# Retention and two expert layers on one core: state product spread over four array quadrants, transposes as quadrant products, PSUM banks in fixed groups, five conversion buffers

## The chip, the core and the metric

The kernel runs on one core of one Trainium2 chip. The engines of the core are TensorE (PE in the profile; PEld is its weight load), VectorE (DVE), ScalarE (ACT), GpSimd (POOL) and SyncE (SP). Here SP only issues DMAs, and POOL issues a second kind of DMA that adds to what stands in memory. The metric is the device time of one execution in microseconds.

## The reference

Inputs are q, k, v of shape (2, 8, 768, 64): 2 sequences, 8 heads, 768 steps, 64 values per head. First comes a retention layer with a 64x64 state per head:

```
gamma = 1 - 2**(-5 - head)
for t in range(768):
    state = gamma * state + outer(k[t], v[t])
    y[t]  = (q[t] @ state) / sqrt(64)
```

Its output, as 1536 rows of 512 values, runs through two expert layers, each with its own weights (512x2048 and 2048x512):

```
h = x @ w_in ;  g = softplus(h)              ;  x = g @ w_out     # first
h = x @ w_in ;  g = h * clip(h+3, 0, 6) / 6  ;  out = g @ w_out   # second
```

q, k and v are 32-bit floats. The expert weights are 64-bit floats and are loaded as pairs of 32-bit words; the products are made in 32-bit formats.

## The kernel before

**Retention.** The 768 steps of a sequence are cut into chunks of 128; a chunk of a sequence is a unit, numbered 0 to 11 (units 0 to 5 are the first sequence). `attend(u)` issues these pieces for a unit, named after the table `cost`:

- Tk and Tq: k and q of the unit are turned so that the 64 values of a head lie on partitions. Two heads (a pair) share one 128x128 transpose, so 4 transposes for k and 4 for q. ACT copies the turned k out of its PSUM bank (`kT`), DVE multiplies the turned q by the decay table into `qT`.
- S: scores of each half chunk (64 steps), 16 products of 64x64 each; DVE masks them into `pt`.
- D: 16 products of k and the scaled v (`vs`) give what each half chunk adds to the state; DVE adds it up into the states `st` at the middle and at the end of the unit.
- C: what the carried state gives to each step, 16 products (8 in the first unit of a sequence). ACT copies the result (`e`).
- I: what the scores give, 16 products; DVE adds the copy of C to it (`g`), and ACT and DVE split the sum into a high and a low part (`x_hi`, `x_lo`) for the first expert layer.

The array of TensorE has 128 rows (partitions that are read) and 128 columns (partitions that are written), and a 64x64 product uses one quarter of it. The head h of a pair lies on partitions 0 to 63 or 64 to 127 by g = h % 2. In S and D the products go round all four quarters. In C before, the state of a head lies on half g and its output on the same half g, so C uses only the two quarters of the diagonal.

**Expert layers.** Both are cut into 3 chunks of 512 tokens and 16 slices of 128 hidden values. G1 of a slice makes h (12 matmuls of 128x512: high x high, high x low, low x high for each of 4 pieces), ACT and DVE make g and split it, and G2 of the slice adds into 4 accumulators (12 matmuls). G2 runs two slices behind G1. In all there are 96 G1 and 96 G2.

**Weights.** A slice's weight is converted once: SP loads its words into one of 3 `raw` buffers, ACT and DVE build the 32-bit value in a converted-word buffer `cv` (4 before), and ACT writes the high part to `w`. The low part comes in one of two ways. For weights chosen by `BY_DVE(n)` DVE subtracts high from full (`w<-cv,w` in the profile). For the others ACT first writes the negative and POOL starts a DMA that adds the full value to what stands in `w`; its `cv` buffer is held until that DMA has landed. The first 32 weights, for the first expert layer, are all needed for its first chunk of tokens.

**Order.** Class `Plan` holds every step as a task with an engine, a cost, its predecessors, a due time and the buffers that it takes and gives back. `Plan.run` simulates the engines with those costs and lays down each engine's instructions in the order that comes out; this order is then fixed, and each engine works through its own list. `spread` says between which G1 and G2 the pieces of units 4 to 11 are due: those of units 4 to 7 from the first G1 on, those of 8 to 11 from the second chunk of tokens on. The 8 PSUM banks are a pool: before, a task that takes two banks gets any two neighbours, other tasks any free ones.

Of the kernel before, what the change touches and what calls it, by code (L numbers as in the profile page):

```python
# [16 lines left out]
P = 128  # L17
# [5 lines left out]
class Plan:  # L23
# [20 lines left out]
    def __init__(self, tc):  # L44
        self.tc, self.tasks, self.pools, self.users, self.slot = tc, [], {}, {}, {}
        self.tensor, self.vector, self.scalar, self.gpsimd, self.sync = (
            self.Engine(self, getattr(tc.nc, e)) for e in ("tensor", "vector", "scalar", "gpsimd", "sync"))
# [13 lines left out]
    def places(self, pool, keys, at=None):  # L61

        times = [(x if at is None else max(x, at), i) for i, x in enumerate(self.pools[pool]) if x is not None]
        if len(keys) == 2:
            have = {i: x for x, i in times}
            two = min(((max(x, have[i + 1]), -i) for i, x in have.items() if i + 1 in have), default=None)
            return two and [-two[1], 1 - two[1]]
        return [i for _, i in sorted(times)[:len(keys)]] if len(times) >= len(keys) else None

    def run(self, log=None):  # L70
        free = {"PE": 0.0, "DVE": 0.0, "ACT": 0.0, "POOL": 0.0, "SP": 1.2}
        line = 0.0
# [52 lines left out]
def kernel(ctx, tc, q, k, v, w1_in, w1_out, w2_in, w2_out, tq, tk, tcc, out):  # L125
# [15 lines left out]
    RAW, CV, LD, LATE = 3, 4, 3, 8  # L141
# [3 lines left out]
    def BY_DVE(n):  # L145
        return n < 6 or n < 2 * NF and n % 3 == 1
# [29 lines left out]
    nc.pool("bank", 8)  # L176
    conv = [[("conv", m, i) for i in range(9)] for m in range(2)]
# [19 lines left out]
    cost = {"Tk": 0.46, "Tq": 0.46, "S": 0.60, "D": 0.60, "C": 0.98, "I": 0.60, "G1": GEMM, "G2": GEMM}  # L197
# [156 lines left out]
    def both(keys):  # L354
        a, b = sorted(nc.slot[x][1] for x in keys)
        return banks[:, a:b + 1:b - a, :NP * HALF].rearrange("p x (n t) -> p x n t", n=NP)

    def sub(keys, j):
        i = sorted(nc.slot[x][1] for x in keys)[j]
        return banks[:, i, :NP * HALF].rearrange("p (n t) -> p n t", n=NP)  # L360

    def bank(key):
        return at_slot(key).rearrange("p (n t) -> p n t", n=NP)
# [4 lines left out]
    def attend(u):  # L368
# [38 lines left out]

        def turned(n):
            def go():
# [4 lines left out]
        tp = task("PE", cost["Tk"], turned("k"), [ik], d["Tk"], take=[("bank", ("kP", u))])  # L414
        kt = task("ACT", ACP, lambda: nc.scalar.activation(tile_of("kT"), bank(("kP", u)), AF.Copy), [tp], d["S"] - 1.0,
                  take=own("kT"), give=[("kP", u)])
        tp = task("PE", cost["Tq"], turned("q"), [iq], d["Tq"], take=[("bank", ("qP", u))], give=[("q", u)])
        qt = task("DVE", PSX, lambda: nc.vector.tensor_tensor(tile_of("qT"), bank(("qP", u)), tq_sb, ALU.mult), [tp, tables["q"]],
                  d["S"] - 1.1, take=own("qT"), give=[("qP", u)])
# [6 lines left out]
        def scores():  # L426
            for p in range(NP):
                for j in range(2):
                    for g in range(2):
                        nc.tensor.matmul(sub(sc, g)[part[j], p, :], tile_of("kT")[part[g], p, part[j]], tile_of("qT")[part[g], p, part[j]])  # L430
# [3 lines left out]
            tile_of("pt").rearrange("p n (g t) -> p g n t", g=2).rearrange("p g n t -> p g n t"), both(sc),  # L434
# [5 lines left out]
        def product():  # L440
            for h in range(H):
                g, p = h % 2, h // 2
                for j in subs:
                    nc.tensor.matmul(sub(ds, j)[part[g], p, :], tile_of("k")[part[j], h, :], tile_of("vs")[part[j], h, :])
# [4 lines left out]
        def middle():  # L449
            if first:  # L450
                nc.vector.tensor_copy(at_slot(mid[1]), sub(ds, 0))
            else:
                nc.vector.tensor_tensor(at_slot(mid[1]), at_slot(("end", u - 1)), sub(ds, 0), ALU.add)
# [3 lines left out]
        if not last:  # L457
            def total():
                nc.vector.tensor_tensor(at_slot(end[1]), at_slot(mid[1]), sub(ds, 1), ALU.add)
# [7 lines left out]

        def carry():
            for j in range(int(first), 2):
                w = at_slot(mid[1] if j else ("end", u - 1))  # L470
                for p in range(NP):
                    for g in range(2):
                        nc.tensor.matmul(bank(("oc", u))[part[g], p, part[j]], w[part[g], p, :], tile_of("qT")[part[g], p, part[j]])

        c = task("PE", cost["C"] / (1 + first), carry, [qt, sm, None if first else ready["end", u - 1]], d["C"],
                 take=[("bank", ("oc", u))], give=[mid[1], ("qT", u)] + ([] if first else [("end", u - 1)]))

        def inner():
            for h in range(H):
                g, p = h % 2, h // 2  # L480
                for j in range(2):
                    nc.tensor.matmul(sub(oi, j)[part[g], p, :], tile_of("vs")[part[j], h, :], tile_of("pt").rearrange(
                        "p n (g t) -> p g n t", g=2)[part[j], g, p, :])
# [6 lines left out]
        def split(t):  # L490
            return t.rearrange("p n (j t) -> p j n t", j=2)

        def of(n):
            return at_slot((n, u)).rearrange("p (n t) -> p n t", n=NP)

        if first:
            o0 = task("ACT", 0.35, lambda: nc.scalar.activation(split(of("on"))[:, 0], sub(oi, 0), AF.Copy), [n], d["I"] + 0.7,
                      take=[("g", ("on", u))], give=oi)
            o1 = task("ACT", 0.35, lambda: nc.scalar.activation(split(of("oe"))[:, 1], split(bank(("oc", u)))[:, 1], AF.Copy), [c],
                      d["I"], take=[("e", ("oe", u))], give=[("oc", u)])  # L500
            on = task("DVE", 0.42, lambda: nc.vector.tensor_tensor(split(of("on"))[:, 1], split(of("oe"))[:, 1], sub(oi, 1), ALU.add),
                      [n, o0, o1], d["I"] + 1.0, give=oi + [("oe", u)])
        else:
            o1 = task("ACT", ACP, lambda: nc.scalar.activation(of("oe"), bank(("oc", u)), AF.Copy), [c],
                      d["I"], take=[("e", ("oe", u))], give=[("oc", u)])
# [115 lines left out]
def _tables(H, S, D):  # L621
# [4 lines left out]
    tq = np.repeat(up.reshape(H // 2, 2, 1, C), D, axis=2).reshape(H // 2, 2 * D, C).transpose(1, 0, 2)  # L626
    tk = gamma[None, :] ** -t[:, None]
    gc = np.repeat((gamma ** C).reshape(H // 2, 2, 1), D, axis=2).reshape(H // 2, 2 * D).T
# [27 lines left out]
```

## Time and profile before

| | |
|---|---|
| runs of the kernel before | 605.39, 607.04, 610.01 us (median 607.04) |
| profiled execution | 606.65 us, of which 604.5 us are the span of the trace |
| PE busy | 582.9 us (96%) |
| DVE, ACT busy | 335.9 us (56%), 304.7 us (50%) |
| granted TensorE clock, mean | 0.992 |

All steps are recorded through one helper, so the rows of the profile carry the line L41; groups are told apart by the tiles that they write and read. `ident,k` is Tk, `ident,q` Tq, `qT,kT` S, `vs,k` D, `qT,st` C and `pt,vs` I. From unit 8 on the tiles lie in the buffers of the weight conversion and are called `raw` and `cv` there: `ident,raw` is T, `cv,raw` D and S, `cv,st` C, `cv,cv` I. The profile counts a 64x64 or 64-column product twice (x32 for 16 products). The chain that ended last is three quarters PE.

### The profile page before, as it was taken

How to read it: one execution, taken by the hardware profiler on the slowest of the kernel's cores; microseconds unless marked ns; L12 is line 12 of the kernel's file. 1: busy time of each engine (PE TensorE's matmuls, PEld its weight loads, DVE VectorE, ACT ScalarE, POOL GpSimd, SP SyncE). 2: the span in 40 equal slices, each digit the busy share in tenths (PEclk: the TensorE clock that was granted, in tenths of full speed). 3: DMA queues.
4: the chain of work that ended last, by engine and by line, in shares of the span. 5: the costliest groups of instructions: out<-in, count | busy, mean ns of one | idle time of the engine just before them, and what ended most of it. 6: DMA issues, size and time to landing. Idle time of an engine off the chain costs nothing.

```text
span 604.5 us, 9654 instructions
## 1 busy us (share of the span) xinstructions
PE 582.9 (96%) x3891; PEld 478.2 (79%) x3891; DVE 335.9 (56%) x584; ACT 304.7 (50%) x516; POOL 44.3 (7%) x57
## 2 busy tenths in 40 slices
PE   7698889999999999999999999999999999999997
PEld 6576668878788888888888887888888888888886
DVE  4899898995655333376677985622422222322223
ACT  2468877994533333476779996622222222222220
POOL 0001111120000000011122221100000000000000
PEclk9899989999999999999999999999999999999999
DMA  8997776966210100046588987510100000100001
GB/s 193 237 252 199 195 183 158 241 180 137 54 37 21 51 0 1 1 105 157 152 196 212 247 211 176 130 18 0 71 1 1 0 1 0 71 0 1 0 1 69
DMA packets 68364, 59.87 MB, mean 99 GB/s; under 512 B 39776, under 2 KB 56416, under 8 KB 68320
## 3 DMA queue, kind: packets, MB, share of 16 engines
q1 hardware_dynamic: 61264, 46.41, 26.9%
q0 software_dynamic: 7056, 12.85, 12.4%
q8 instruction: 30, 0.49, 0.4%
q14 instruction: 14, 0.11, 0.1%
HBM read 43.26 MB, written 3.15 MB: 77 GB/s over the span
## 4 chain that ended last, share of the span: by engine, by line
PE 76%; DVE 10%; DMA 6%; ACT 5%; issue 3%; SPq 1%; DVEq 0%; ACTq 0%
PE banks L41 76%; DVE cv L41 5%; DMA raw<-in_moe_w_out_dram 3%; DMA raw<-in_moe_w_in_dram 2%; DVE raw L41 1%; ACT w L41 1%; DVE g L41 1%; DVE lo L41 1%; ACT raw L41 1%; DMA v<-in_v_dram 1%; ACT cv L41 1%; ACT e L41 1%; SPq L41 1%; DVE x_lo L41 1%; DVE w L41 1%
## 5 line engine op out<-in xcount | busy, mean ns | idle before, releaser
L41 PE MATMUL banks<-x_hi,w 128*128 128x512 f32 x768 | 254.8, 393 | 5.0 <-ACT kT L41 2.2
L41 PEld LDWEIGHTS banks<-x_hi,w 128*128 128x128 f32 x768 | 144.8, 189 | 37.1 <-DVE g L41 2.5
L41 PE MATMUL banks<-x_lo,w 128*128 128x512 f32 x384 | 150.2, 391 | 0.0
L41 PE MATMUL banks<-hi,w 128*128 128x512 f32 x384 | 127.5, 393 | 0.8 <-ACT w L41 0.5
L41 PE MATMUL banks<-w,hi 128*128 128x512 f32 (+1 forms) x386 | 118.3, 388 | 0.0
L41 DVE SCALAR_TENSOR_TENSOR g<-e,banks 128x512 f32<-128x512 f32 x48 | 33.0, 688 | 114.1 <-ACT e L41 114.0
L41 ACT ACTIVATE e<-banks,three 128x512 f32<-128x512 f32 x48 | 32.9, 686 | 124.6 <-PE banks L41 116.7
L41 DVE SCALAR_TENSOR_TENSOR cv<-raw,cv 128x512 uint32<-128x512 uint32 x128 | 87.5, 689 | 6.7 <-ACT cv L41 4.2
L41 DVE TENSOR_TENSOR lo<-g,hi 128x512 fp32r<-128x512 f32 x96 | 66.2, 690 | 44.7 <-ACT hi L41 43.4
L41 ACT ACTIVATE hi<-g 128x512 fp32r<-128x512 f32 x96 | 60.5, 630 | 49.8 <-DVE g L41 33.3
L41 PEld LDWEIGHTS banks<-hi,w 128*128 128x128 f32 x384 | 72.0, 188 | 17.0 <-ACT w L41 0.9
L41 PEld LDWEIGHTS banks<-x_lo,w 128*128 128x128 f32 x384 | 72.6, 189 | 14.7
L41 PEld LDWEIGHTS banks<-w,hi 128*128 128x128 f32 x386 | 72.4, 188 | 14.9
L41 ACT ACTIVATE w<-cv 128x512 fp32r<-128x512 f32 x113 | 68.3, 624 | 16.7 <-DVE cv L41 16.2
L41 PE MATMUL banks<-lo,w 128*128 128x512 f32 x192 | 75.1, 391 | 1.4 <-DVE lo L41 1.4
L41 PE MATMUL banks<-w,lo 128*128 128x512 f32 (+1 forms) x193 | 74.9, 388 | 0.0
L41 POOL DMA_DIRECT2D w<-cv x49 | 43.3, 887 | 348.9 <-ACT w L41 208.3
L41 ACT ACTIVATE g<-banks 128x512 f32<-128x512 f32 (+1 forms) x50 | 29.2, 584 | 54.7 <-PE banks L41 54.2
L41 ACT ACTIVATE raw<-raw 128x512 f32<-128x512 f32 x64 | 42.7, 667 | 8.7 <-DMA raw<-in_moe_w_out_dram 5.1
L41 PEld LDWEIGHTS banks<-lo,w 128*128 128x128 f32 x192 | 36.0, 188 | 9.5 <-DVE lo L41 2.2
L41 DVE SCALAR_TENSOR_TENSOR g<-g,e 128x512 f32<-128x512 f32 x48 | 33.1, 690 | 16.3 <-ACT e L41 15.7
L41 PEld LDWEIGHTS banks<-w,lo 128*128 128x128 f32 x193 | 36.3, 188 | 7.5
(58 smaller groups left out, 340.2 us busy)
## 6 DMA issues: line engine op xcount, KB each, us to landing
raw<-in_moe_w_in_dram SPq DMA_DIRECT2D x32, 512.0 KB, 4.1
raw<-in_moe_w_out_dram SPq DMA_DIRECT2D x32, 512.0 KB, 4.3
w<-cv POOLq DMA_DIRECT2D x49, 256.0 KB, 4.4
out_dram<-e SPq DMA_DIRECT2D x11, 256.0 KB, 2.0
q<-in_q_dram SPq DMA_DIRECT2D x8, 256.0 KB, 5.0
v<-in_v_dram SPq DMA_DIRECT2D x8, 256.0 KB, 4.9
k<-in_k_dram SPq DMA_DIRECT2D x7, 256.0 KB, 4.7
raw<-in_k_dram SPq DMA_DIRECT2D x4, 256.0 KB, 3.2
```

The costliest lines, as they stand in the source:

```text
L41: return self.plan.tc.keep_in_program_order(getattr(self.engine, op)(*args, **kwargs))
```

## The change

Five things change together:

1. **Halves.** In odd pairs the two heads change halves: `row(h)` says on which half of the partitions the turned k, the turned q and the state of head h lie; the tables `tq` and `tc` are rolled to match. The output of C and I stays on half h % 2. So C's products go round all four quarters, and its result lies in two banks, by the pair's parity.
2. **Transposes.** Tk and Tq are no 128x128 transposes any more: each head and each half chunk is a 64x64 product with the identity, 16 for k and 16 for q. Both go to one pair of banks, k in the first halves of the banks, q in the second.
3. **Banks.** `bank_groups` gives h banks 0 and 1, the accumulators 4 to 7 as one group, and every piece of the retention the pair 2 and 3 (units 0 to 3 may also take the other pairs).
4. **Conversion.** There are 5 `cv` buffers instead of 4, and `BY_DVE` takes every fourth weight instead of every third from the seventh on: 12 weights instead of 15 go the DVE way, 20 instead of 17 of the first 32 the POOL way.
5. **Planner.** The costs of T and C and the spacing in `spread` change (C and I are due in separate gaps), and the DMA model lets the queues of SP and POOL run side by side.

```diff
-    RAW, CV, LD, LATE = 3, 4, 3, 8
+    RAW, CV, LD, LATE = 3, 5, 3, 8
     def BY_DVE(n):
-        return n < 6 or n < 2 * NF and n % 3 == 1
+        return n < 6 or n < 2 * NF and n % 4 == 1
...
+    def bank_groups(keys):
+        kind, u = keys[0][0], keys[0][-1]
+        if kind == "h":
+            return [[0], [1]]
+        if kind == "acc":
+            return [[4, 5, 6, 7]]
+        return [[2, 3]] + ([[4, 5], [6, 7], [0, 1]] if u < START else [])
...
-    cost = {"Tk": 0.46, "Tq": 0.46, "S": 0.60, "D": 0.60, "C": 0.98, "I": 0.60, "G1": GEMM, "G2": GEMM}
+    cost = {"Tk": 0.56, "Tq": 0.56, "S": 0.58, "D": 0.58, "C": 0.58, "I": 0.58, "G1": GEMM, "G2": GEMM}
...
-            for i, block in enumerate(([("Tk", u), ("Tq", u)], [("D", u)], [("S", u)], [("C", u), ("I", u)])):
-                gaps.setdefault(start + int((4 * n + i) * per), []).extend(block)
-    spread(range(START, FIRST), 0, 1.0)
+            for i, block in enumerate(([("Tk", u), ("Tq", u)], [("D", u)], [("S", u)], [("C", u)], [("I", u)])):
+                gaps.setdefault(start + int((5 * n + i) * per), []).extend(block)
+    spread(range(START, FIRST), 0, 0.8)
...
             if t.load:
-                line = max(line, end + 1.2) + t.load
-                end = line + 0.5
+                other = "SP" if t.eng == "POOL" else "POOL"
+                begin = max(line[t.eng], end + 1.2)
+                shared = max(0.0, min(t.load, line[other] - begin))
+                line[t.eng] = begin + t.load + shared
+                line[other] += shared
+                end = line[t.eng] + 0.5
...
+    def row(h):
+        return (h + h // 2) % 2
...
-                for p in range(NP):
-                    nc.tensor.transpose(bank((n + "P", u))[:, p, :], tile_of(n)[:, 2 * p:2 * p + 2, :].rearrange("s h d -> s (h d)"), ident)
+                for h in range(H):
+                    for j in range(2):
+                        nc.tensor.matmul(quad(tp, j, x)[part[row(h)], h // 2, :], tile_of(n)[part[j], h, :], ident[part[j], part[j]])
...
         def carry():
             for j in range(int(first), 2):
                 w = at_slot(mid[1] if j else ("end", u - 1))
-                for p in range(NP):
-                    for g in range(2):
-                        nc.tensor.matmul(bank(("oc", u))[part[g], p, part[j]], w[part[g], p, :], tile_of("qT")[part[g], p, part[j]])
+                for h in range(H):
+                    p, r = h // 2, row(h)
+                    nc.tensor.matmul(crossed()[part[h % 2], p % 2, p // 2, part[j]], w[part[r], p, :], tile_of("qT")[part[r], p, part[j]])
```

The planner lays down other orders with this. The first place is TensorE at the end of unit 3, ahead of the first G1 (its first row reads `x_hi` and `w`). Before:

```order
L41 MATMUL banks<-pt_0_134,vs_0_132 64x64 x16
L41 MATMUL banks<-ident,k_1_124 128x128 x4
L41 MATMUL banks<-ident,q_1_121 128x128 x4
L41 MATMUL banks<-ident,q_2_122 128x128 x4
L41 MATMUL banks<-vs_0_132,k_1_124 64x64 x16
L41 MATMUL banks<-x_hi_66,w_79 128x512
```

With the change:

```order
L41 MATMUL banks<-pt_0_135,vs_0_133 64x64 x16
L41 MATMUL banks<-ident,k_1_125 64x64 x16
L41 MATMUL banks<-ident,q_1_122 64x64 x16
L41 MATMUL banks<-vs_1_134,k_1_125 64x64 x16
L41 MATMUL banks<-x_hi_66,w_80 128x512
```

The transpose of the next unit's q (`q_2`) no longer stands ahead of the first G1, and D of unit 4 (`vs_1,k_1`) now needs the pair of banks that T of unit 4 has just filled.

The second place is TensorE in the second chunk of tokens, at unit 9; `cv_0,raw_2` is S, the two rows `cv_0,st` are C, `cv_2,cv_1` is I. Before:

```order
L41 MATMUL banks<-x_hi_67,w_84 128x512
L41 MATMUL banks<-cv_0_75,raw_2_74 64x64 x16
L41 MATMUL banks<-cv_0_75,st_137 64x64 x8
L41 MATMUL banks<-cv_0_75,st_136 64x64 x8
L41 MATMUL banks<-cv_2_77,cv_1_76 64x64 x16
L41 MATMUL banks<-hi_109,w_87 128x512
```

With the change:

```order
L41 MATMUL banks<-lo_112,w_87 128x512
L41 MATMUL banks<-hi_109,w_87 128x512
L41 MATMUL banks<-cv_0_75,st_138 64x64 x8
L41 MATMUL banks<-cv_0_75,st_137 64x64 x8
L41 MATMUL banks<-x_hi_67,w_88 128x512
L41 MATMUL banks<-x_lo_70,w_88 128x512
```

S, C and I, which stood together, now stand alone, each between two G1 or G2.

The third place is DVE from the low part of unit 3's output (`x_lo`) to the first step on the fourth weight (`TENSOR_SCALAR raw_0`). Before:

```order
L41 TENSOR_TENSOR x_lo_69<-g_105,x_hi_66 128x4x128
L41 TENSOR_TENSOR w_81<-cv_2_77,w_81 128x512
L41 TENSOR_TENSOR qT_0_130<-banks,tq_sb 128x512
L41 TENSOR_TENSOR st_138<-st_138,small 128x256
L41 TENSOR_TENSOR st_136<-st_138,banks 128x256
L41 TENSOR_TENSOR st_137<-st_136,banks 128x256
L41 TENSOR_TENSOR vs_1_133<-v_2_128,small 128x512
L41 TENSOR_TENSOR qT_1_131<-banks,tq_sb 128x512
L41 TENSOR_TENSOR st_137<-st_137,small 128x256
L41 TENSOR_SCALAR raw_0_72<-raw_0_72 128x512
```

With the change:

```order
L41 TENSOR_TENSOR x_lo_69<-g_106,x_hi_66 128x4x128
L41 TENSOR_TENSOR qT_0_131<-banks,tq_sb 128x2x4x64
L41 TENSOR_TENSOR w_82<-cv_2_77,w_82 128x512
L41 TENSOR_TENSOR vs_0_133<-v_2_129,small 128x512
L41 TENSOR_TENSOR st_137<-st_139,banks 128x256
L41 TENSOR_SCALAR raw_0_72<-raw_0_72 128x512
```

Four fewer rows stand between the two, and unit 4's q comes ahead of the weight's low part.

## Rows read from the trace of the kernel before

**Rows 1.** Busy time of the engines in three stretches, us from the start.

```profile
core 0: us, PE busy (x) PEld busy (x) DVE busy (x) ACT busy (x) POOL busy (x), PEclk, DMA share, GB/s
33.90:90.30 56.40, 49.66 (x503) 38.47 (x496) 52.83 (x99) 44.86 (x80) 7.48 (x8) 0.97 0.80 206
90.30:147.50 57.20, 55.75 (x359) 45.22 (x358) 49.04 (x90) 45.59 (x80) 7.83 (x9) 1.00 0.73 180
147.50:205.00 57.50, 57.49 (x709) 46.74 (x707) 30.54 (x54) 22.55 (x38) 0.00 (x0) 1.00 0.21 52
```

**Rows 2.** Timeline of PE: start us, us, instruction, [idle before, releaser]; seven waits.

```profile
52.87 0.50 PE L41 MATMUL banks<-hi,w 128*128 128x512 f32 x1 [0.46 <-ACT w L41]
53.94 0.73 PE L41 MATMUL banks<-hi,w 128*128 128x512 f32 x2 [0.34 <-DVE w L41]
...
57.72 0.50 PE L41 MATMUL banks<-x_hi,w 128*128 128x512 f32 x1 [1.23 <-ACT g L41]
...
62.61 1.08 PE L41 MATMUL banks<-qT,st 64*64 64x64 f32 x29 [1.12 <-ACT g L41]
...
68.78 0.50 PE L41 MATMUL banks<-x_hi,w 128*128 128x512 f32 x1 [1.13 <-DVE g L41]
...
86.16 0.69 PE L41 MATMUL banks<-x_hi,w 128*128 128x512 f32 x1 [2.20 <-ACT kT L41]
...
90.69 0.69 PE L41 MATMUL banks<-vs,k 64*64 64x64 f32 x32
...
128.54 0.50 PE L41 MATMUL banks<-lo,w 128*128 128x512 f32 x1 [1.45 <-DVE lo L41]
```

**Rows 3.** Timeline of PE, unit 9: T, D, and S, C, I between G1 and G2.

```profile
162.63 0.39 PE L41 MATMUL banks<-hi,w 128*128 128x512 f32 x1
162.86 1.03 PE L41 MATMUL banks<-ident,raw 128*128 128x128 f32 x8
163.65 0.48 PE L41 MATMUL banks<-x_hi,w 128*128 128x512 f32 x1
163.97 0.40 PE L41 MATMUL banks<-x_lo,w 128*128 128x512 f32 x1
...
168.96 0.39 PE L41 MATMUL banks<-hi,w 128*128 128x512 f32 x1
...
169.91 0.50 PE L41 MATMUL banks<-x_hi,w 128*128 128x512 f32 x1
170.24 0.39 PE L41 MATMUL banks<-x_lo,w 128*128 128x512 f32 x1
...
172.85 0.69 PE L41 MATMUL banks<-cv,raw 64*64 64x64 f32 x32
173.37 1.11 PE L41 MATMUL banks<-cv,st 64*64 64x64 f32 x32
174.36 0.69 PE L41 MATMUL banks<-cv,cv 64*64 64x64 f32 x32
```

**Rows 4.** Timeline of PE: the first matmul of the first G1.

```profile
33.91 0.50 PE L41 MATMUL banks<-x_hi,w 128*128 128x512 f32 x1
```

**Rows 5.** Timeline of DVE, from unit 3's low part to the fourth weight.

```profile
33.20 0.69 DVE L41 TENSOR_TENSOR x_lo<-g,x_hi 128x512 fp32r<-128x512 f32 x1
...
34.41 0.68 DVE L41 TENSOR_TENSOR qT<-banks,tq_sb 128x512 f32<-128x512 f32 x1
...
37.93 0.42 DVE L41 TENSOR_SCALAR raw<-raw 128x512 f32<-128x512 f32 x1
```

**Rows 6.** Groups of DVE and ACT instructions to 150 us: shapes, count | busy, mean ns | idle before.

```profile
L41 DVE TENSOR_TENSOR w<-cv,w 128x512 fp32r<-128x512 f32 x15 | 10.3, 684 | 0.1
L41 DVE TENSOR_TENSOR pt<-banks,small 128x512 f32<-128x512 f32 x8 | 5.5, 687 | 1.8 <-PE banks L41 1.7
...
L41 ACT ACTIVATE w<-cv 128x512 fp32r<-128x512 f32 x49 | 30.0, 625 | 9.1 <-DVE cv L41 9.0
L41 ACT ACTIVATE cv<-raw,half 128x512 uint32<-128x512 uint32 x24 | 18.3, 763 | 1.8 <-DMA w<-cv 1.8
```

More of the change, by code (lines that the diff above doesn't have):

```diff
@@ L61, in places @@
     def places(self, pool, keys, at=None):
[L63 to L68, printed above, removed]
+        times = {i: x if at is None else max(x, at) for i, x in enumerate(self.pools[pool]) if x is not None}
+        if pool in self.groups:
+            ok = [g for g in self.groups[pool](keys) if all(i in times for i in g)]
+            return min(ok, key=lambda g: max(times[i] for i in g), default=None)
+        return sorted(times, key=lambda i: (times[i], i))[:len(keys)] if len(times) >= len(keys) else None
     def run(self, log=None):
         free = {"PE": 0.0, "DVE": 0.0, "ACT": 0.0, "POOL": 0.0, "SP": 1.2}
-        line = 0.0
+        line = {"SP": 0.0, "POOL": 0.0}
         todo = {e: sorted((t for t in self.tasks if t.eng == e), key=lambda t: (t.due, t.n)) for e in free}
@@ L176 @@
     nc.pool("bank", 8)
+    def bank_groups(keys):
[5 more added lines that the diff above has]
+        return [[2, 3]] + ([[4, 5], [6, 7], [0, 1]] if u < START else [])
+    nc.groups["bank"] = bank_groups
     conv = [[("conv", m, i) for i in range(9)] for m in range(2)]
@@ L352, in table, with both, quad, split @@
         return nc.add("SP", 0.45, lambda: nc.sync.dma_start(out=dst, in_=src), [], when, load=1.3 if dst is tq_sb else 0.1)
[L354 to L363, printed above, removed]
+    def both(keys, x=0):
+        a = nc.slot[keys[0]][1]
+        return banks[:, a:a + 2, x * NP * HALF:(x + 1) * NP * HALF].rearrange("p j (n t) -> p j n t", n=NP)
+    def quad(keys, j, x=0):
+        return banks[:, nc.slot[keys[j]][1], x * NP * HALF:(x + 1) * NP * HALF].rearrange("p (n t) -> p n t", n=NP)
+    def split(t):
+        return t.rearrange("p n (j t) -> p j n t", j=2)
+    def row(h):
+        return (h + h // 2) % 2
     part = [slice(j * HALF, (j + 1) * HALF) for j in range(2)]
@@ L406, in attend @@
             tables["c"] = table(tc_sb, tcc, begin + 3.1)
+        tp = [("tp", j, u) for j in range(2)]
         def turned(n):
+            x = "kq".index(n)
             def go():
-                for p in range(NP):
-                    nc.tensor.transpose(bank((n + "P", u))[:, p, :], tile_of(n)[:, 2 * p:2 * p + 2, :].rearrange("s h d -> s (h d)"), ident)
-            return go
[L414 to L419, printed above, removed]
+                for h in range(H):
+                    for j in range(2):
+                        nc.tensor.matmul(quad(tp, j, x)[part[row(h)], h // 2, :], tile_of(n)[part[j], h, :], ident[part[j], part[j]])
+            return go
+        tk_ = task("PE", cost["Tk"], turned("k"), [ik], d["Tk"], take=[("bank", x) for x in tp])
+        kt = task("ACT", ACP, lambda: nc.scalar.activation(split(tile_of("kT")), both(tp, 0), AF.Copy), [tk_], d["S"] - 1.0,
+                  take=own("kT"), give=tp)
+        tq_ = task("PE", cost["Tq"], turned("q"), [iq, tk_], d["Tq"], give=[("q", u)])
+        qt = task("DVE", PSX, lambda: nc.vector.tensor_tensor(split(tile_of("qT")), both(tp, 1), split(tq_sb), ALU.mult),
+                  [tq_, tables["q"]], d["S"] - 1.1, take=own("qT"), give=tp)
         vs = task("DVE", TT, lambda: nc.vector.tensor_tensor(
@@ L428, in scores @@
                 for j in range(2):
[L429 to L430 removed]
+                    for r in range(2):
+                        nc.tensor.matmul(quad(sc, r)[part[j], p, :], tile_of("kT")[part[r], p, part[j]], tile_of("qT")[part[r], p, part[j]])
         s = task("PE", cost["S"], scores, [kt, qt], d["S"], take=[("bank", x) for x in sc], give=[("kT", u)])
         pt = task("DVE", PSX, lambda: nc.vector.tensor_tensor(
[L434 removed]
+            split(tile_of("pt")), both(sc),
             mask.rearrange("p (a n t) -> p a n t", a=1, n=1).to_broadcast([P, 2, NP, HALF]), ALU.mult), [s],
@@ L458, in total @@
             def total():
-                nc.vector.tensor_tensor(at_slot(end[1]), at_slot(mid[1]), sub(ds, 1), ALU.add)
+                nc.vector.tensor_tensor(at_slot(end[1]), at_slot(mid[1]), quad(ds, 1), ALU.add)
             def faded():
@@ L466, in attend, with crossed @@
             ready["end", u] = task("DVE", 0.42, faded, [e, tables["c"]], due["C", u + 1] - 2.0, give=[end[1]])
+        oc = [("oc", x, u) for x in range(2)]
+        def crossed():
+            a = nc.slot[oc[0]][1]
+            return banks[:, a:a + 2, :NP * HALF].rearrange("p x (n t) -> p x n t", n=NP // 2)
         def carry():
@@ L470, in carry @@
                 w = at_slot(mid[1] if j else ("end", u - 1))
-                for p in range(NP):
-                    for g in range(2):
-                        nc.tensor.matmul(bank(("oc", u))[part[g], p, part[j]], w[part[g], p, :], tile_of("qT")[part[g], p, part[j]])
+                for h in range(H):
+                    p, r = h // 2, row(h)
+                    nc.tensor.matmul(crossed()[part[h % 2], p % 2, p // 2, part[j]], w[part[r], p, :], tile_of("qT")[part[r], p, part[j]])
         c = task("PE", cost["C"] / (1 + first), carry, [qt, sm, None if first else ready["end", u - 1]], d["C"],
-                 take=[("bank", ("oc", u))], give=[mid[1], ("qT", u)] + ([] if first else [("end", u - 1)]))
+                 take=[("bank", x) for x in oc], give=[mid[1], ("qT", u)] + ([] if first else [("end", u - 1)]))
         def inner():
             for h in range(H):
-                g, p = h % 2, h // 2
                 for j in range(2):
-                    nc.tensor.matmul(sub(oi, j)[part[g], p, :], tile_of("vs")[part[j], h, :], tile_of("pt").rearrange(
-                        "p n (g t) -> p g n t", g=2)[part[j], g, p, :])
+                    nc.tensor.matmul(quad(oi, j)[part[h % 2], h // 2, :], tile_of("vs")[part[j], h, :], split(tile_of("pt"))[part[j], row(h), h // 2, :])
         n = task("PE", cost["I"], inner, [pt, vs], d["I"], take=[("bank", x) for x in oi], give=[("pt", u), ("vs", u)])
```

29 lines of the change are left out of this document (14 added, 15 removed).

## The prediction

> **What bounds the kernel now.** I read the busy time by stretches first, then the waits of TensorE in its timeline, then the timeline of one unit between two matrix products, and last the groups of DVE and ACT. From 147.5 us on TensorE is never idle (57.49 of 57.50 us in the first stretch behind it), while DVE and ACT are half empty [rows 1]; there only a shorter list on TensorE moves the end. From the first G1 at 33.91 us [rows 4] to 147.5 us TensorE and DVE are both nearly full: DVE is busy for 52.83 of 56.40 us and then for 49.04 of 57.20 us, ACT for 44.86 and 45.59 us [rows 1]. Here TensorE waits seven times: 0.46 + 0.34 + 1.23 + 1.12 + 1.13 + 2.20 + 1.45 = 7.9 us, each time for ACT or DVE [rows 2]. After the 2.20 us the twelve matmuls of one G1 take from 86.16 to 90.69 us, 4.5 us [rows 2]; at one matmul each 0.23 us (162.63 to 162.86 [rows 3]) they would take 2.8 us. That is the lower of the clock's two levels for most of that G1 (mean granted clock 0.97 in that stretch [rows 1]) and costs 1.7 us. So 9.6 us are lost in this phase, and that is all there is to win in it. Ahead of 33.9 us the loads of q, k, v and of the first weights set the pace; the change leaves their order as it is up to the sixth load after unit 3's k, so I count that part as unchanged until unit 3's pieces are done.
>
> **TensorE's own list.** Prices come from unit 9 [rows 3]. D alone between two products: from the last matmul ahead (168.96) to the first behind (169.91) and from that to the next (170.24), 0.95 + 0.33, less two steps of 0.23: 0.82 us. S with another group behind it: 172.85 to 173.37, 0.52. So standing alone costs 0.30 more than standing in a row. C before: 173.37 to 174.36, 0.99, nearly twice S with as many products: with all four quarters in use I price it like S, 0.52 in a row, 0.82 alone. T before: 162.86 to 163.65 and 0.32 - 0.23 behind it, 0.88 us, and nothing ahead, since the step into it is 0.23. T after: two groups of 16 quadrant products, 0.52 + 0.82 = 1.34.
> The Trainium skill says, in "TensorEngine Tiling (Array Packing)", Key Properties, that a change of the tiling mode drains TensorE, while going from tile to tile doesn't. The trace agrees: 0.32 us into D, 0.23 into the full-size T. By that rule turning T into 64x64 products and setting C and I apart each add drains; were they free, the late term below would be 0.6 us less for each of its three full units.
>
> *Late, units 8 to 11.* Before, units 9 to 11 take T 0.88, D 0.82 and S, C, I in one row 0.52 + 0.99 + 0.82 = 2.33; with the change T 1.34, D 0.82, and S, C, I alone 3 x 0.82 = 2.46. That is 0.46 + 0.13 = 0.59 us more a unit. In unit 8 only C and I stood together: 0.46 + 2.46 - (0.82 + 0.99 + 0.82) = 0.29. Sum 3 x 0.59 + 0.29 = **+2.1 us**, all on the path, for nothing covers TensorE there.
>
> *Early, units 4 to 7 behind the first G1.* Nine stretches of pieces become eighteen: 9 x 0.30 = 2.7. C saves 0.47 in units 4, 5 and 7 and half in unit 6: -1.65. One group of unit 5's transposes (0.52) no longer stands ahead of the first G1. Together **+1.6**.
>
> *The first G1.* D of unit 4 stands ahead of it and now needs the pair of banks that T of unit 4 fills, so it waits for kT (ACT) and qT (DVE). DVE has unit 3's x_lo at 33.20, and qT directly behind it; its steps are 0.60 apart (33.20 to 34.41 are two) [rows 5]. qT ends at about 34.5, D takes 0.6, and G1 starts near 35.1 instead of 33.91: **+1.2**.
>
> **DVE, ACT and the queues.** On DVE four rows fewer stand between that x_lo and the fourth weight: x_lo, qT, a low part, vs (four steps of 0.60) and one state sum (half as wide, put at the 0.42 of the last row): 36.0 us instead of 37.93 [rows 5], 1.9 earlier. Three weights go the POOL way instead: three DVE subtractions fewer, 3 x 0.60 = 1.8 of DVE's time (their own length is 0.684 [rows 6]). So DVE's chain comes **3.7 us earlier** to the end of the first chunk. ACT gets three copies more, 3 x 0.625 = 1.9 [rows 6]; they lie in the 23 us that ACT has free in the two stretches [rows 1], and if they don't, 1.9 of the 3.7 come off. POOL gets three DMAs more on a queue that is busy for 15.3 of 113.6 us [rows 1]. The fifth cv buffer is worth between nothing and the one wait of 1.8 us that ACT had for a buffer which such a DMA held [rows 6]; I take nothing. kT, qT and the copy of C now read two banks at once; `pt` always did and takes 0.687 us for 512 values [rows 6], like qT with 0.68 [rows 5], so I take nothing. The halves changing places cost no instruction. With two banks for h, a third G1 waits until ACT has emptied the first; with a G2 or a piece between them that is 2.7 us or more, and I take nothing; what it costs without that cover is in the second rival.
>
> **The sum** goes against the profiled execution, 606.65 us. At the least TensorE gains what DVE gains at its last wait: -3.7 + 2.1 = -1.6, 605.0. At the most all 9.6 us of waits and low clock go, against 1.6 + 1.2 of its own: -9.6 + 2.8 + 2.1 = -4.7, 601.9. For that the phase of 113.6 us would have to shrink to 106.8 with 101.9 - 1.8 = 100.1 us of DVE work in it, 94%: as full from end to end as DVE is in its fullest stretch (52.83 of 56.40 [rows 1]). I take the middle, 603.5. The median of the runs is 0.4 above the profiled execution; so **603.9 us**. A measurement of this kernel can tell about 1% from no change: 601.0 to 613.1 us.
>
> **The rivals.**
> 1. *Nothing waits any more, and the first G1 is not late.* If TensorE becomes the only bound, and the pair of banks is free in time, the 1.2 go too: 606.65 - 9.6 + 1.6 + 2.1 = 600.8, 601.2 against the median; with T groups that overlap better than S does, 600. For it: five of the seven waits lie ahead of 90 us, where DVE is 1.9 us ahead at once. Against it: ACT, which released four of them, gets more to do.
> 2. *The bank pair becomes the new wait (the slow side).* Every piece of units 4 to 7 uses banks 2 and 3, so a piece can start only when DVE or ACT has emptied the one before, and both work through fixed lists in which that step stands behind weight steps. TensorE then waits with G1 and G2 queued behind the piece. The price of one such wait is that of the waits for ACT's kT and g, 1.1 to 2.2 us [rows 2]. It decides from the point where the emptying step starts more than one G1 (2.7 us) after its piece. If the old waits stay as well, the end is 606.65 + 1.6 + 1.2 + 2.1 = 611.6, and with two or three new ones 614 to 617; if DVE's lead pays for part of them, 605.5 to 611.
> 3. *C stays slow.* The Trainium skill says, in the same page under PSUM Pressure, that different row tiles can't use one PSUM bank at the same time. C writes both of its banks from both row halves. By that rule C's groups would go one after another, as mechanism of this kernel: C stays at 0.99. Four late units pay 4 x 0.47 = 1.9 more and the early ones up to 1.65: 605.4 to 607, 606 to 607.5 against the median. Rows speak against it: S's 0.52 for as many products as C's 0.99 is what two quarters against four give, and C before already wrote one bank from both row halves without being slower than half of S [rows 3].
>
> **Chances.** The forecast (602.3 to 605.4 against the median) 0.47; rival 1 0.18, of which 0.13 below 601.0; rival 2 0.27, of which 0.08 above 613.1; rival 3 0.08. So faster by over 1% 0.13, within 1% 0.79, slower 0.08. The range takes in the forecast, rival 3, most of rival 1 and rival 2 up to one new wait on top of half the old ones: 600 to 610, with 0.2 outside.
>
> **What would show it.** In the profile of the changed kernel: `cv,st` takes about 0.5 us from its start to the next piece or product (rival 3: 1.0); T takes 1.1 to 1.2 us; from the start of unit 8 on, four units take 2 us more of TensorE than before; the first G1 starts near 35 us, behind a wait of D for DVE's qT; between it and the end of the first chunk TensorE's waits sum to 2 to 6 us instead of 7.9 and no G1 runs at the low clock; DVE's fourth weight starts near 36 us. The prediction is wrong if waits in front of 64x64 pieces, released by kT, qT, st, pt or e, sum to more than 3 us (rival 2), or if TensorE has no wait over 0.5 us behind 40 us (rival 1).

## The result, and the profile after

The changed kernel takes 616.05 us (median of 4 runs, 615.95 to 617.05) against 607.21 us of the kernel before in the same series: ratio 1.0145, 95% interval 1.0105 to 1.0186. The prediction, 603.9 us with a range of 600 to 610, was wrong, and so was its sign. The profiled execution took 616.13 us, its span is 614.1 us.

One row places the loss: the first G1 starts at 43.46 us, against 33.91 [rows 4]. From there to the end both kernels take the same: 614.1 - 43.46 = 570.6 and 604.5 - 33.91 = 570.6 us. So 9.55 us are lost ahead of the first G1, the part that the prediction counted as unchanged but for 1.2 us.

TensorE's timeline of the changed kernel in that part. Each row gives start, duration, instruction, number of records, and in brackets the idle time before it and its releaser. A record is one matmul in the trace; a 64x64 product shows as two.

```profile
15.38 0.68 PE L41 MATMUL banks<-ident,k 64*64 64x64 f32 x29
17.68 0.27 PE L41 MATMUL banks<-ident,k 64*64 64x64 f32 x2 [1.62 <-issue]
...
20.37 0.68 PE L41 MATMUL banks<-qT,kT 64*64 64x64 f32 x28 [0.52 <-DVE qT L41]
23.71 0.37 PE L41 MATMUL banks<-qT,kT 64*64 64x64 f32 x2 [2.65 <-issue]
...
27.05 1.13 PE L41 MATMUL banks<-ident,k 64*64 64x64 f32 x27
29.00 0.37 PE L41 MATMUL banks<-ident,k 64*64 64x64 f32 x3 [0.82 <-issue]
...
32.22 1.13 PE L41 MATMUL banks<-vs,k 64*64 64x64 f32 x32 [1.89 <-DVE g L41]
34.70 1.13 PE L41 MATMUL banks<-qT,kT 64*64 64x64 f32 x32 [1.34 <-DVE qT L41]
...
38.90 1.13 PE L41 MATMUL banks<-ident,k 64*64 64x64 f32 x32 [0.89 <-DVE g L41]
...
42.40 1.13 PE L41 MATMUL banks<-vs,k 64*64 64x64 f32 x32 [1.52 <-DVE qT L41]
43.46 0.79 PE L41 MATMUL banks<-x_hi,w 128*128 128x512 f32 x1
```

Read the first pairs: TensorE stops in the middle of a group, after 29 of its 32 records, and goes on with the same group later. The releaser is "issue": the profile shows no event that the group waited for. From one stop to the next there are 127 records, counted with the rows left out here. The first stop, behind record 349 of the program, stands in the transpose of unit 2's k, the second in S of unit 2, the third in the transpose of unit 3's k. The kernel before has one such stop, behind record 350, in C of unit 2:

```profile
18.32 0.33 PE L41 MATMUL banks<-qT,st 64*64 64x64 f32 x2
19.41 0.97 PE L41 MATMUL banks<-qT,st 64*64 64x64 f32 x26 [0.76 <-issue]
```

TensorE's waits up to the first G1, by releaser (total us, times, longest); after:

```profile
PE banks L41 <- issue: 5.1, 3, 2.7
PE banks L41 <- DVE qT L41: 4.7, 5, 1.5
PE banks L41 <- DVE g L41: 2.8, 2, 1.9
```

and before:

```profile
PE banks L41 <- DVE cv L41: 4.0, 1, 4.0
PE banks L41 <- DVE qT L41: 1.3, 3, 0.8
PE banks L41 <- issue: 0.8, 1, 0.8
```

The stops grow by 4.3 us, the waits for qT by 3.4 and those for g by 2.8, while the 4.0 us that TensorE stood before unit 3's k are gone; with the small ones that is some 6.5 us. TensorE's busy time makes up the rest: 27.84 us up to 43.40 against 24.66 us up to 33.90, for 864 records instead of 588, at a mean granted clock of 0.73 instead of 0.90. The granted clock is 0.50, the lower of its two levels (1.2 GHz), from 23.2 to 47.1 us in the changed kernel and from 24.9 to 31.7 us in the kernel before; in both it fell while TensorE stood longest (2.65 and 4.03 us).

One profile of a startup is not exact to the microsecond. The kernel before and four profiles of kernels that share its startup (the carry runs below) have the first G1 at 33.91, 33.45, 33.14, 36.48 and 35.64 us, and their one stop at 0.76, 1.20, none, 0.85 and 0.74 us. So 9.55 us are clear of that spread, and differences under some 3 us at the first G1 are not.

The three stretches of [rows 1] in the changed kernel:

```profile
33.90:90.30 56.40, 51.63 (x736) 39.76 (x736) 49.17 (x92) 40.68 (x73) 6.27 (x7) 0.88 0.72 183
90.30:147.50 57.20, 56.65 (x466) 44.32 (x459) 52.81 (x100) 51.05 (x92) 11.65 (x13) 1.00 0.81 204
147.50:205.00 57.50, 56.94 (x752) 43.94 (x754) 29.97 (x53) 22.68 (x38) 0.00 (x0) 1.00 0.22 48
```

All waits of TensorE from 43.5 to 155 us, where the kernel before had the seven of [rows 2] (7.9 us):

```profile
PE banks L41 <- ACT w L41: 0.8, 1, 0.8
PE banks L41 <- DVE lo L41: 0.7, 3, 0.3
PE banks L41 <- DVE w L41: 0.3, 1, 0.3
```

And unit 9 on TensorE, which answers to [rows 3]: T and C, each alone between two products, and the start of D:

```profile
171.31 0.39 PE L41 MATMUL banks<-x_hi,w 128*128 128x512 f32 x1
171.63 1.16 PE L41 MATMUL banks<-ident,raw 64*64 64x64 f32 x64
172.72 0.50 PE L41 MATMUL banks<-hi,w 128*128 128x512 f32 x1
173.06 0.39 PE L41 MATMUL banks<-lo,w 128*128 128x512 f32 x1
...
175.67 0.69 PE L41 MATMUL banks<-cv,raw 64*64 64x64 f32 x32
...
182.50 0.39 PE L41 MATMUL banks<-hi,w 128*128 128x512 f32 x1
182.82 0.69 PE L41 MATMUL banks<-cv,st 64*64 64x64 f32 x32
183.44 0.50 PE L41 MATMUL banks<-x_hi,w 128*128 128x512 f32 x1
183.78 0.39 PE L41 MATMUL banks<-x_lo,w 128*128 128x512 f32 x1
```

T costs 172.72 - 171.31 + 0.34 - 0.46 = 1.29 us, C alone 0.94 + 0.34 - 0.46 = 0.82.

### The profile page after: what moved, and what is told of

Same layout as the page of the kernel before. It is cut to its first block, busy times and chain, and to the rows that moved or that the text cites. A ratio compares the mean times of both kernels' runs of the same rounds, so it can differ in the third digit from the quotient of the medians.

```text
span 614.1 us, 11002 instructions
## 1 busy us (share of the span) xinstructions
PE 590.5 (96%) x4563; PEld 479.0 (78%) x4563; DVE 335.2 (55%) x581; ACT 305.7 (50%) x519; POOL 46.9 (8%) x60
## 4 chain that ended last, share of the span: by engine, by line
PE 67%; issue 8%; DMA 8%; DVE 8%; ACT 8%; POOL 1%; DVEq 0%; POOLq 0%; ACTq 0%
PE banks L41 67%; DVE cv L41 3%; DMA raw<-in_moe_w_in_dram 3%; DMA raw<-in_moe_w_out_dram 3%; ACT w L41 2%; ACT raw L41 1%; ACT cv L41 1%; POOL w L41 1%; DMA w<-cv 1%; ACT e L41 1%; DVE g L41 1%; DMA k<-in_k_dram 1%; ACT hi L41 1%; DVE lo L41 1%; DVE raw L41 1%
## 5 line engine op out<-in xcount | busy, mean ns | idle before, releaser
L41 ACT ACTIVATE w<-cv 128x512 fp32r<-128x512 f32 x116 | 70.1, 624 | 8.3 <-DVE cv L41 8.1
L41 POOL DMA_DIRECT2D w<-cv x52 | 45.8, 881 | 355.9 <-ACT w L41 211.0
```

Of the source, the lines that this page charges most:

```text
L41: return self.plan.tc.keep_in_program_order(getattr(self.engine, op)(*args, **kwargs))
```

## The experiments

Two theories for the 9.55 us. The code excerpts are shortened; "..." marks what is left out. **A:** TensorE's program itself comes late. The transposes of one unit's k are 32 records as 64x64 products where full ones are 4; the program is brought in pieces while the loads fill the DMA engines, and the waits behind the stops follow from them. **B:** the shared pair of banks and the new order: D of unit 3, T and D of unit 4 wait until a pair is emptied, and q's transpose stands behind k's.

**Full transposes in the changed kernel.** The heads change halves in the load instead.

```diff
-  for h in range(H):
-      for j in range(2):
-          matmul(quad(tp, j, x)[part[row(h)], h // 2, :], tile_of(n)[part[j], h, :], ident[part[j], part[j]])
+  for p in range(NP):
+      transpose(whole(x)[:, p, :], tile_of(n)[:, 2 * p:2 * p + 2, :], ident)
   ...
   # load of k and q
-  dma_start(out=tile_of(n), in_=src)
+  dma_start(out=tile_of(n)[:, :4], in_=src[:, :4])
+  for g in range(2):
+      dma_start(out=tile_of(n)[:, 5 - g::2], in_=src[:, 4 + g::2])
   ...
```

> The changed kernel, but every transpose of k and q is again four products of 128x128, as before; heads 4 to 7 (instead of those of the odd pairs) change halves, and they change them in the load (three DMAs for k and q instead of one). Order of TensorE, banks and waits as in the changed kernel. TensorE's records ahead of the first G1 fall from 864 to 584 (588 before the change). Theory A (the program itself comes late: TensorE stops three times in the middle of a group, 1.62 + 2.65 + 0.82 us, each 127 records apart, and everything behind it shifts): at most one stop of under 1 us, first G1 at 34 to 36 us instead of 43.46, median 605 to 608 us. Theory B (the shared pair of banks and the new order: waits for g, qT and kT): first G1 stays at 42 to 44 us, median 614 to 616.

607.08 us, ratio to the kernel before 1.0012 (0.9987 to 1.0037): the loss is gone. DVE and ACT work through the same lists as in the changed kernel. No stop with the releaser "issue" is left, as A says. The first G1 is later than A had it:

```profile
26.10 1.10 PE L41 MATMUL banks<-ident,k 128*128 128x128 f32 x4 [5.27 <-DMA k<-in_k_dram]
...
33.95 0.65 PE L41 MATMUL banks<-ident,k 128*128 128x128 f32 x4 [1.33 <-DVE g L41]
...
37.23 0.79 PE L41 MATMUL banks<-x_hi,w 128*128 128x512 f32 x1
```

So 6.2 of the 9.55 us go with the transposes; in the other 3.3 stand unit 3's k, which comes 1.0 us later than before with its three DMAs, and the wait for g by which unit 4 gets its pair (B's). These 3.3 us are no more than the spread of one startup. From the first G1 to the end this kernel takes 606.1 - 37.23 = 568.9 us, 1.7 less than the changed kernel; that is the rest of what it gains.

**The transposes alone, in the kernel before.**

```diff
-  for p in range(NP):
-      transpose(bank((n + "P", u))[:, p, :], tile_of(n)[:, 2 * p:2 * p + 2, :], ident)
+  for h in range(H):
+      for j in range(2):
+          matmul(sub(pair, j)[part[h % 2], h // 2, :], tile_of(n)[part[j], h, :], ident[part[j], part[j]])
   ...   # k's and q's transposes each take a pair of banks of their own
```

> The kernel before, with one thing changed: a transpose is sixteen 64x64 products into a pair of banks of its own (k's pair and q's pair apart), so 896 records ahead of the first G1 instead of 588. Nothing else of the change. Theory A (program late): stops in mid-group of 4 to 6 us in all ahead of the first G1, which comes at 40 to 44 us instead of 33.91; median 612 to 617, with 2 us of it late, in units 8 to 11. Theory B (shared pair and order): no stops beyond the one of 0.76, first G1 at 34 to 35.5, median 608 to 610.

613.44 us, ratio 1.0118 (1.0086 to 1.0150). The waits up to the first G1, which starts at 40.48 us:

```profile
PE banks L41 <- issue: 8.4, 5, 3.8
PE banks L41 <- ACT kT L41: 1.9, 3, 0.9
```

```profile
40.48 0.50 PE L41 MATMUL banks<-x_hi,w 128*128 128x512 f32 x1
```

This one edit, with no shared pair, moves the first G1 by 6.6 us and brings five stops, 127 or 128 records apart (between the last two, twice that). The lists of DVE and ACT are those of the kernel before up to 61.8 us, so none of the new order is in it. A's place and sign hold; its 4 to 6 us of stops were too few.

**Half the records.** A transpose as eight products of 128 rows by 64 columns.

```diff
-  matmul(quad(tp, j, x)[part[row(h)], h // 2, :], tile_of(n)[part[j], h, :], ident[part[j], part[j]])
+  matmul(whole(x)[part[row(h)], h // 2, :], tile_of(n)[:, h, :], ident)
   ...
```

> The changed kernel, but a transpose is eight products of 128 rows by 64 columns instead of sixteen of 64x64: half the records (704 ahead of the first G1 instead of 864). Order, banks and waits as in the changed kernel. Theory A (program late): in proportion to the records, 864 gave 43.46 and 588 gave 33.91, so 37.9 us for the first G1 (36.5 to 39.5), the stops in mid-group sum to 1.5 to 3 us instead of 5.1, median 609 to 612. Theory B (banks and order): first G1 at 42 to 44, median 614 to 616.

The first G1 comes at 39.96 us, the stops sum to 2.3 us: between the changed kernel and the one with full transposes, as A has it, though 0.5 us beyond its bound. The time, 614.73 us, is not as A had it. These products are longer, at the full clock too,

```profile
168.03 1.97 PE L41 MATMUL banks<-ident,raw 128*64 128x128 f32 x32
```

1.97 us for a unit's two transposes against 1.16, and from T to T a late unit takes 187.16 - 168.03 = 19.13 us instead of 18.33.

**Any pair for unit 4.**

```diff
-  return [[2, 3]] + ([[4, 5], [6, 7], [0, 1]] if u < START else [])
+  return [[2, 3]] + ([[4, 5], [6, 7], [0, 1]] if u <= START else [])
```

> The changed kernel, but unit 4, too, may take any free pair of banks (units 0 to 3 may already), so that its transposes need not wait for unit 3's pair and its D not for its own transposes. Theory A (program late): stops in mid-group stay at 4 to 6 us; only the waits of 0.89 and 1.52 us go, so the first G1 comes at 41 to 43.5 us; median 613 to 616. Theory B (banks): these waits were what the pair cost, and DVE moves up with them: first G1 at 36 to 40, median 606 to 612.

614.83 us (ratio 1.0147), first G1 at 42.67 us. The two waits of unit 4 (0.89 and 1.52 us) are gone, the stops are there, 6.9 us in all and so 1.8 more than in the profile of the changed kernel. The first G1 comes 0.8 us earlier (1.4 with S of unit 4, 0.63 us, which now stands ahead of it); that is inside the spread of one startup, so the price of the pair can't be read from it. In the time nothing shows, against the 606 to 612 us that B expected.

**Why the program comes late.** The same TensorE program up to the last transpose ahead of the first G1 (D of unit 4 comes behind it), with few loads beside it; the lists of DVE and ACT differ from 22 us on, since the weights come later:

```diff
   ...
   # fetch
+  if u == START - 1:
+      return
   # load
-  return task("SP", 0.45 * parts, fetch(n, parts), [], when, ...)
+  return task("SP", 0.45 * parts, fetch(n, parts), [ready.get("I2")], when, ...)
   # behind unit 2's I, which is task n
+  ready["I2"] = n
+  for f in order:
+      T["F", f].after.append(n)
   ...
```

> The changed kernel with TensorE's program as it is, but few loads while units 1 to 3 run: unit 3's q, k and v are left out (it works on what lies in its buffers, so the output is wrong), and all weights and the loads of units 4 and later wait for unit 2's last group. From about 14 us until then the DMA engines have next to nothing to do. The time itself says nothing; the stops in mid-group do. Theory A1 (a piece of the program, 127 records long, waits behind the data on the DMA engines): the stop in S of unit 2, 2.65 us in the changed kernel, is under 0.7 us, and those before I of unit 2 sum to under 2 us instead of 4.3. Theory A2 (a piece takes some 5 us to come whatever else the DMA engines do): the stop in S of unit 2 stays at 2 us or more.

```profile
15.47 0.67 PE L41 MATMUL banks<-ident,k 64*64 64x64 f32 x29
18.04 0.27 PE L41 MATMUL banks<-ident,k 64*64 64x64 f32 x2 [1.90 <-issue]
...
21.17 1.18 PE L41 MATMUL banks<-qT,kT 64*64 64x64 f32 x30
22.05 0.34 PE L41 MATMUL banks<-vs,k 64*64 64x64 f32 x2
...
25.71 0.27 PE L41 MATMUL banks<-ident,k 64*64 64x64 f32 x2 [0.21 <-issue]
```

Busy times from 17 to 26 us, with the DMA engines' share in the last column but one; here:

```profile
17.00:26.00 9.00, 7.12 (x272) 6.31 (x274) 5.95 (x12) 2.34 (x5) 0.00 (x0) 0.81 0.14 31
```

and in the changed kernel:

```profile
17.00:26.00 9.00, 4.93 (x195) 4.34 (x196) 4.04 (x8) 2.89 (x5) 0.00 (x0) 0.84 1.01 261
```

The stop of 2.65 us in S of unit 2 is gone, that of 0.82 is 0.21 (a further one, 128 records behind it, is 0.40): A1. Ahead of it there are two stops still (1.22 and 1.90 us, 3.1 in all where under 2 was expected): the DMA engines, meant to be free from 14 us on, were half busy until 17 us (0.56). The packets of TensorE's program show the pace: in the changed kernel they lie at 15.4, 21.0 and 26.4 us, here at 15.5, 19.4, 23.1 and 26.8, one each 3.7 to 3.8 us instead of 5.3 to 5.6. The granted clock was 0.5 around 21 us here as well, so TensorE asked a little later than at the full clock; the piece was there at 22.0, 4.0 us behind the one before, against 6.0 with the loads.

**Is something in the change worth keeping?** Two parts alone and together, the startup left as it was:

```diff
   # buffers_only
-  RAW, CV, LD, LATE = 3, 4, 3, 8                  n % 3 == 1
+  RAW, CV, LD, LATE = 3, 5, 3, 8                  n % 4 == 1     (and the new load lines of the plan)
   ...
   # carry_only: units 6 to 11 load k and q with heads 4 to 7 swapped, and the swapped q table
-  matmul(bank(("oc", u))[part[g], p, part[j]], ...)
+  matmul(crossed()[part[h % 2], p // 2, p % 2, part[j]], w[part[row(h)], p, :], ...)
   ...   # the plan prices C of these units at 1 / 1.7 of before, and C takes two banks
```

> The kernel before with the parts of the change that are not TensorE's: five buffers for converted words, every fourth instead of every third weight by DVE, and the new rule by which the plan shares the load line. Transposes, banks and C as before. If the change's gain behind the first G1 comes from DVE's lighter list: first G1 at 33.5 to 34.5 us, waits of TensorE between it and 147 us 3 to 6 us instead of 7.9, median 602.5 to 604.5 against 605.5 for the kernel before. Rival (DVE was not what TensorE waited for in the end; the carry gave the gain): 605 to 607.

> The kernel before with only the carry changed, and only in the second half (units 6 to 11): there heads 4 to 7 change halves in the load (three DMAs for k and for q, the q table loaded a second time, swapped), and C writes two banks from four quadrants. Transposes stay 128x128, the startup is word for word that of before. If C in four quadrants takes 0.52 us instead of 0.99 and nothing else changes: 4 x 0.47 = 1.9 us less behind unit 8, median 603 to 604.5 against 605.5. Rival (C needs a second bank, and what it gains is waited for elsewhere): 605 to 608.

> Both of the above together: everything of the change except the transposes in quadrants, the fixed banks and the separate places for C and I, with the carry's new form only from unit 6 on. If the program's late coming in the startup was all that the change lost: first G1 near 34 us, no stop in mid-group over 0.8 us, median 601 to 603.5, faster than both kernels. Rival (something else of the change costs): 605 or more.

The buffers: 606.46 us, ratio 1.0002 (0.9967 to 1.0037), nothing; that is the rival's number. TensorE's waits from the first G1 to 147 us fall from 7.9 to 6.0 us, and in the rest of the program 2.5 us of waits for g stand where before there were 0.3. The carry: 602.96 us, **0.9945 (0.9916 to 0.9975)**, faster than both kernels. Both: 605.35 us, 0.9974 (0.9949 to 1.0000). That is the rival's number too: the first G1 comes at 33.41 us and no stop is left, yet the kernel takes 2.4 us more than with the carry alone, a difference that the intervals do not keep apart. And the carry's gain is not where it was expected: unit 8 starts at 143.71 us instead of 147.51, and from there to the end it takes 457.1 us where the kernel before takes 457.0. TensorE's waits between the first G1 and 147 us are 4.5 us there instead of 7.9. Three more runs on that:

```diff
   # carry_slow
-  for h in (0, 1, 4, 5, 2, 3, 6, 7):
+  for h in (0, 2, 1, 3, 5, 7, 4, 6):
   # carry_two_quarters
-  to = crossed()[part[h % 2], p // 2, p % 2, part[j]]
+  to = crossed()[part[r], p // 2, p % 2, part[j]]
```

> The kernel with only the carry changed (from unit 6 on), every instruction of every engine in the same order but one: within C the heads come so that neighbouring products fall on the same quarter. C should take 1.0 us or more again instead of 0.5. If C's length is what made the kernel 0.5% faster (602.96 against 607.2 in that series): at least half of the gain goes, ratio to the kernel before 0.998 or more. Rival (C's length was not it; the order that the plan found and the waits it avoids ahead of unit 8 were): the ratio stays at 0.993 to 0.997, and the start of unit 8 stays near 143.7 us.

> The kernel with only the carry changed, once more, beside the one with the slow order of heads: ratio 0.992 to 0.998 if the first series was no accident of its chip; with the order of heads deciding, 1 to 3 us less than the other.

> The kernel with only the carry changed (from unit 6 on), every instruction in the same order, but C of units 6 to 11 writes each head to the rows of the half that it comes from, so that it again uses two quarters of the array and not four (heads 4 to 7 of the second half come out exchanged in the carry's share; that part of the output is wrong). The slow order of heads left C at 0.51 us; this must bring it back to about 0.99. Theory: C's length is on the path in the late units, 4 x 0.47 = 1.9 us, and hidden in units 6 and 7: ratio to the kernel before 0.997 to 0.999, half of the gain gone. Rival (the gain is the plan's other order ahead of unit 8 alone): ratio 0.993 to 0.996 as it was.

The order of heads did not make C longer (0.51 us in unit 8 still), so that run, 0.9935 (0.9911 to 0.9958), tells nothing of C's length; the repetition gave 0.9946 (0.9924 to 0.9969). With two quarters, unit 8's C is long again:

```profile
159.65 1.08 PE L41 MATMUL banks<-cv,st 64*64 64x64 f32 x29
160.53 0.27 PE L41 MATMUL banks<-cv,cv 64*64 64x64 f32 x1
```

against, with four,

```profile
154.63 0.69 PE L41 MATMUL banks<-cv,st 64*64 64x64 f32 x32
155.14 0.65 PE L41 MATMUL banks<-cv,cv 64*64 64x64 f32 x32
```

and the ratio is 0.9939 (0.9915 to 0.9964), no different. (The execution that was profiled, 608.02 us, is the longest of the eleven; a stretch at a granted clock of 0.5 from 72.0 to 78.8 us lies in it, so it does not show where the others gain.) C's own shortening doesn't show in the time: in units 9 to 11 I stands 0.76 us behind C in place of 0.87, 0.16 us a unit (15.09 and 15.25 us from T to T). There I, with C in four quarters, has to wait:

```profile
169.43 0.69 PE L41 MATMUL banks<-cv,st 64*64 64x64 f32 x32
170.19 0.69 PE L41 MATMUL banks<-cv,cv 64*64 64x64 f32 x32
```

The profile puts 0.20 us of idle time of the weight load ahead of this I down to ACT's g, which ends at 170.13 us. So the 0.5% are not C's length. What is left is the order that the plan finds when C's price, its second bank and the extra loads are in it; that this order gives the gain is argued from what the runs rule out. Which of the plan's moves would do it was not tried.

## Why the prediction was wrong, point by point

**The step that failed** is the one in "What bounds the kernel now": that ahead of 33.9 us the loads set the pace and the part is unchanged until unit 3's pieces are done. The loads did set TensorE's pace, but also by way of its program, and the change puts 276 more records there. The prediction priced 32 records of transposes at 0.52 us, at the rate of S in unit 9, and put nothing for bringing the program. In unit 9 no stop is seen; 512-column products of 0.23 us each stand between the groups there. In the startup TensorE went on behind its stops each 5.3 to 6.0 us, 127 records further. The first G1 came 8.35 us later than the 1.2 us that the prediction allowed, and so beyond 613.1 us, to which it gave a chance of 0.08. A warning stood in the trace of before: one stop of 0.76 us in mid-group. Shown by experiment: putting the transposes in costs 6.6 us at the first G1, taking them out gives 6.2 back, and the stop of 2.65 us goes when the loads go.

**What follows the stops.** With TensorE late in unit 2, DVE stands idle and then does everything at once; its timeline in the changed kernel:

```profile
24.23 0.69 DVE L41 TENSOR_TENSOR pt<-banks,small 128x512 f32<-128x512 f32 x1 [2.81 <-PE banks L41]
...
27.02 0.42 DVE L41 TENSOR_SCALAR raw<-raw 128x512 f32<-128x512 f32 x1
```

In the kernel before the first weight's step comes at 20.86 us:

```profile
20.86 0.43 DVE L41 TENSOR_SCALAR raw<-raw 128x512 f32<-128x512 f32 x1 [1.14 <-ACT raw L41]
```

It stands behind `pt` of unit 2 in DVE's list and comes at 27.02 us with the change. These are the "fixed lists" of rival 2, but set off by the program and not by the banks. The longer stretch at the lower clock (23.2 to 47.1 us) comes with the stops too; what the late lists and the clock each take of the 9.55 us was not separated.

**The first G1, +1.2.** The mechanism was right: D of unit 4 waits for qT (1.52 us). What it costs by itself is not shown, as freeing it moved the first G1 by 0.8 us, less than one startup varies.

**TensorE's own list.** Right. T 1.29 us for 1.34, C and D alone 0.82; a late unit takes 18.33 us with five G1 or G2 where it took 15.01 with four. One of them is 2.73 us: 18.33 - 15.01 - 2.73 = 0.59 more, as forecast. C in four quarters is fast; rival 3 fell. The Trainium skill's rule behind that rival ("TensorEngine Tiling (Array Packing)", PSUM Pressure) shows no price here: in unit 8 of the carry run I stands 0.51 us behind C.

**Behind the first G1** TensorE waits 1.8 us instead of 7.9, and one G1 still runs at the low clock, from 43.46 to 48.07, about 1.8 us over: -9.6 + 3.6 = -6.0. Against it stand +1.6 and +2.1 of its own, a wait of 0.56 ahead of unit 8's D, and one of 1.6 between 300 and 400 us in place of 0.3: -0.4, where 0.0 was measured. The forecast's middle stands for 603.5 - 606.65 - 1.2 = -4.35 us here, so this part failed too. It took some 8 us of the 9.6 as recovered, where 6.0 were, and it put the 1.9 us of new waits behind unit 8 at nothing, TensorE being its only bound there. Its terms for TensorE's longer list hold: up to unit 8 the changed kernel takes 111.94 us instead of 113.60, with one G1 more in it, and -1.66 - 2.73 + 6.0 = 1.6. Of the seven waits six, not five, lie ahead of 90 us. The DVE term (-3.7) can't be told from the late start; by itself it is worth nothing measurable (buffers_only).

**Rivals.** Rival 1 fell: TensorE still has waits of 0.85, 0.56 and 1.6 us behind 48 us. Rival 2's price (614 to 617) was met, and so was its sign: the waits for kT, qT and pt sum to 6.2 us ahead of the first G1 (2.3 before). But with the waits of unit 4's pair gone the time stays, and with the full transposes in the same pair the loss goes; so the banks were not the main reason.

## What to carry to other kernels

Count instructions, not only their time. Where many short matmuls stand close together and loads fill the DMA engines, TensorE can run out of program, as here, where it took 3.4 us for the 127 records between two stops and the next piece came 5.6 us behind the last. A transpose that becomes four small products, eight records for one, then costs more than its array time. A row that stops in the middle of a group with the releaser "issue" is the sign; look for it in the profile of before, and compare records per us there. One stop of that kind also came and went between executions of one startup, so look at more than one profile. And when a plan orders the work, an edit's gain may be the new order's: hold the order fixed and change the price alone before crediting the edit.

## What the runs showed of the hardware

- TensorE stopped for its program at distances of 127 or 128 matmul records, or twice that, with as many weight loads beside them, in five kernels. The places are the same whatever piece stands there: behind record 222, 349 or 350, 476 or 477, 603 to 605, 732 and 859. Each of the 35 packets of the program's queue carries 0.57 MB / 35 = 16 KB, first the changed kernel, then the one before:

```profile
q8 instruction: 35, 0.57, 0.4%
q8 instruction: 30, 0.49, 0.4%
```

  The number of packets goes with the matmuls at 127 for one: 4563 / 127 = 35.9 and 3891 / 127 = 30.6.

- A packet lies each 3.7 to 3.8 us where the data leave the DMA engines free (share 0.14) and each 5.3 to 5.6 us where they are full (1.01). TensorE goes on 2.2 to 3.1 us behind it, at every stop of the six kernels that have one up to here (the kernel before and the five).
- The Trainium skill ("Runtime: NRT & Kernel Launch", Instruction fetch mechanics) says that the program is fetched in blocks of 16 KiB, 256 instructions, and that crossing a block is mostly hidden. The distance of 127 matmuls with their weight loads agrees; hidden it was not, at 5.1 us in the changed kernel and 8.4 in the one with the transposes alone.
- The order of the products within C made no difference (0.51 us from C to I of unit 8 and 0.76 in units 9 to 11, in both orders); which quarters they use did (0.88 and 0.87 in two).
- One startup program gave the first G1 at 33.14 to 36.48 us in five profiled executions.
